# A scan feeding a routed expert layer on one core: weights loaded in smaller transfers, and four pieces of work placed later in the program

## The chip, the core and the metric

The kernel runs on one core of a Trainium2 chip. The metric is the device time of one execution in microseconds (us), and the smaller number is better. Three executions of the kernel before took 277.38, 278.45 and 274.22 us, so the median is 277.38 us.

## The reference, cut to what matters

Two layers follow each other. The first is a chunked linear scan over 768 positions for 4 batches and 8 heads, with a state of 16 x 32 per head:

```python
for c in range(nc):
    cum = np.cumsum(la, axis=-1)
    L = np.exp(cum[:, :, :, None] - cum[:, :, None, :]) * causal
    M = np.einsum('bhin,bhjn->bhij', Cc, Bc) * L
    y_intra = np.einsum('bhij,bhjd->bhid', M, xc)
    y_inter = np.einsum('bhin,bhnd->bhid', Cc, state) * np.exp(cum)[:, :, :, None]
    y[:, :, sl] = y_intra + y_inter
    state = decay_full * state + sum_j(Bc * xc * decay_from_j)
```

Its output is laid out as 3072 tokens of 256 numbers. The second layer sends every token to one of 8 experts by a cosine score, and runs that expert's two matrices:

```python
logits = normalized(x) @ normalized(expert_emb).T / tau
expert_idx = np.argmax(logits, axis=1)
gate_w = softmax(logits)[expert_idx]
for e in range(E):
    mask = expert_idx == e
    h = np.maximum(x[mask] @ w1[e], 0.0)        # 256 -> 1024
    out[mask] = gate_w[mask, None] * (h @ w2[e]) # 1024 -> 256
```

All of it is in float32.

## The kernel before, in words

**First layer, function `mamba`.** The positions are cut into 6 chunks of 128; a chunk with 2 of the 4 batches is a pair, so there are 12 pairs, and the loop `for i in range(2, NP)` (line 478) takes one pair an iteration, in an order that is written out by hand and kept as written on every engine. In iteration `i` the matrix engine (PE) spreads the decays of pair `i+2` (L270), multiplies B by C of pair `i` (`inner`, L329), turns the outputs of pair `i-2` into tokens with their scores (`finish`, L404), adds up states (L292), and makes the outputs of pair `i-1` (`outputs_before` L362, `outputs_within` L377). VectorE (DVE) multiplies C by the decays (`scale_c`, L281: it reads the PSUM tile `pz` that `finish` writes next), masks the products (`keep_inner`, L338), and picks the experts (`pick`, L626 to L635; `locate`, L654 to L658, gives each token its row). GpSimd (POOL) writes tokens to their experts' rows in HBM by indirect DMA (`scatter`, L669), up to four a call.

The decays of chunks 4 and 5 are computed by the generator `decays` (L111), whose five portions run on DVE: one before the loop (L476) and one at the end of each of iterations 2 to 5 (L526). The second portion's result is turned at iteration 5 (`turn_decays`, L141), and the last portion's is needed at iteration 6 (`between`, L149).

**Second layer, function `moe`.** Each expert has 416 places for tokens (4 tiles of 104), in rows in HBM. Expert 0 is treated apart: its first 208 places, from chunks 0 to 3, are the early tokens (`load_early`, tile `xe`), multiplied with `up` (L831) while the last tokens are still being scattered, at the end of `mamba` (lines 535 to 549). `moe` (lines 1108 to 1118) then runs `down` (L848) for the early tokens, `out` (L862, then an indirect DMA from POOL, L869), then `part(1)`, the other 208 places of expert 0 (tile `xg`), and then `part(2)` to `part(8)`, one for each of experts 1 to 7. These seven use a scheme with seven products instead of eight (class `Seven`). It needs mixtures of the weights, made on POOL by four additions of 128 x 512 each (L890): `mix_up` for the first matrix and `mix_down` for the second. A copy into the tile `tick` (L1103) makes POOL wait for the gate of the current part before it mixes.

`prepare` (L789 to L800) turns scores into gates: nine small DVE instructions and one exponential on ScalarE (ACT). It is called for the early tokens at the end of `mamba` (L549), ahead of `down`.

`leftover_blocks` (L1121 to L1176) lays out blocks for tokens beyond an expert's 416 places: 23 DVE instructions, all issued between `out` of the early tokens and `part(1)`. `leftover` (L1179) runs such blocks later if there are any.

**PSUM in `up` and `down`.** A tile `sum` has 5 buffers (L823). In `up`, odd `f` are evacuated by DVE (`hT`, L837) and even `f` by ACT (L835). `down` for `j = 0` reads `hT` of `f = 0, 1, ... 7` in turn.

**Weights.** Each expert has `w1` (1 MB) and `w2` (1 MB), in pools of 3 buffers. `load_w1` (L226) issues four transfers from the sync engine (SP), each to 32 partitions with two runs of 4 KB each; `w2` is one transfer to 128 partitions. All loads are issued from SP, whose queue is in program order: the loads of `mamba`, weights of experts 0 and 1 (L488), `xe` (waits for the last scatter of chunk 3), weights of expert 2 (L527), and the two `xg` (wait for the last scatter of all).

Of the kernel before, what the change touches and what calls it, by code (L numbers as in the profile page):

```python
# [24 lines left out]
TR, NT = 104, 4  # L25
# [199 lines left out]

def load_w1(k, t, w1):  # L226

    w = w1.rearrange("(t j o d) f -> o t d j f", t=2, j=2, o=2)
    for o in range(2):
        for i in range(2):  # L230
            p = 32 * (2 * o + i)
            k.nc.sync.dma_start(t[p : p + 32], w[o, i])


def load_weights(k, e):
    k.w1t[e] = k.wp.tile([128, KD, F], F32, name="w1", tag="w1")
    load_w1(k, k.w1t[e], k.w1[e])
    k.w2t[e] = k.wp.tile([128, KF, DM], F32, name="w2", tag="w2")
    k.nc.sync.dma_start(k.w2t[e][:], k.w2[e].rearrange("(f p) m -> p f m", p=128))


def pair(k, p):
# [122 lines left out]
            )  # L365


def outputs_within(k, p):

    c, b, t = pair(k, p)  # L370
    s = k.un[p]
    for i in range(2):
        for q in range(4):
            for v in range(2):
                n = 32 * (4 * v + q)
                o = 64 * (q % 2) + 32 * v
                k.nc.tensor.matmul(  # L377
                    half_of(k, p, q // 2, i)[o : o + 32, :], lhsT=s.x[:, i, n : n + 32], rhs=s.g[i][:, q, v, :],
                    start=(c == 0 and i == 0), stop=True, tile_position=(0, o), skip_group_check=True,
                )  # L380
# [36 lines left out]
def mamba(k):  # L417
    k.f = k.mc.tile([128, 2, Q], F32, name="f")
    k.r = k.mc.tile([128, 2, Q], F32, name="r")
    k.rT = k.mc.tile([128, 2, 128], F32, name="rT")  # L420
    k.parts = k.mc.tile([128, 2, 2, 4], F32, name="parts")
    k.tick = k.const.tile([1, 1], F32, name="tick")
    k.sides = k.mc.tile([128, NB, 2, 8], F32, name="sides")
    k.whole = k.mc.tile([128, 2, NB, NC - 1], F32, name="whole")
    k.old, k.V, k.yT, k.to = {}, {}, {}, {}
    k.dec = [decays(k, kk) for kk in range(2)]
    NP = NU // 2
    load_decays(k)
    load(k, 0)
    load_emb(k)  # L430
    build_consts(k)
    load(k, 1)
    load(k, 2)
    fill_rows(k)
    load(k, 3)
    for _ in range(4):
        next(k.dec[0])
    turn_decays(k, 0, k.py[:, 384:512])

    for p in range(2):  # L440
        spread_f(k, p)
        scale_c(k, p)
        if p:
            next(k.dec[0])
        else:
            measure_emb(k)
        scale_x(k, p)
    scale_x(k, 2)
    sums(k, 0)
    spread_f(k, 2)  # L450
    scale_c(k, 2)
    scale_emb(k)

    inner(k, 0)
    sums(k, 1)
    between(k, 0, k.pf[:, 256:288])
    turn_emb(k)
    spread_f(k, 3)
    for j in range(2):
        keep_inner(k, 0, j)  # L460
    states(k, 0)
    join(k, 0, k.pf[:, 256:288])
    next_states(k, 0)
    scale_x(k, 3)
    scale_c(k, 3)
    route_consts(k)
    inner(k, 1)
    sums(k, 2)
    sums(k, 3)
    outputs_within(k, 0)  # L470
    for j in range(2):
        keep_inner(k, 1, j)
    keep_outputs(k, 0)
    states(k, 1)
    scale_x(k, 4)
    next(k.dec[1])  # L476

    for i in range(2, NP):
        new = i + 2 if i + 2 < NP else None
        out, done = i - 1, i - 2  # L480
        c = (i + 2) // 2

        pick_now = (i - 3) // 2 if i % 2 else None
        place_now = i // 2 - 2 if i % 2 == 0 and 4 <= i else None
        if i % 2 == 0 and i // 2 + 3 < NC:
            load(k, i // 2 + 3)
        if i in (6, 2 * EC + 2):
            load_weights(k, len(k.w1t))  # L488
        if new is not None:
            spread_f(k, new)  # L490
            scale_c(k, new)
        inner(k, i)
        if i == 5:
            turn_decays(k, 1, k.py[:, 384:512])
        if i == 6:
            between(k, 1, k.py[:, 304:336])
            join(k, 1, k.py[:, 304:336])
        if place_now is not None:
            locate(k, place_now)
            if place_now == EC - 1:  # L500
                count_early(k)
        for j in range(2):
            keep_inner(k, i, j)
        if place_now == EC - 1:
            split_early(k)
            scatter(k, place_now, 0, NB, None)
            load_early(k)
        elif 4 <= i < 2 * EC + 2:
            scatter(k, (i - 4) // 2, 2 * (i % 2), 2, done)
        if i % 2 == 0 and i // 2 < NC - 1:  # L510
            next_states(k, i // 2)
        finish(k, done)
        keep_tokens(k, done)
        if new is not None and c < NC - 1:
            sums(k, new)
        outputs_before(k, out)
        outputs_within(k, out)
        keep_outputs(k, out)
        if pick_now is not None:
            pick(k, pick_now)  # L520
        if new is not None and i % 2 and c < NC - 1:
            states(k, c)
        if new is not None and new + 1 < NP:
            scale_x(k, new + 1)
        if i < 6:
            next(k.dec[1])  # L526
    load_weights(k, len(k.w1t))  # L527
    last = NP - 1
    outputs_before(k, last)
    outputs_within(k, last)  # L530
    locate(k, NC - 2)
    finish(k, last - 1)
    keep_outputs(k, last)
    keep_tokens(k, last - 1)
    j = k.early[0]
    j.turn_x(k.pf[:])
    finish(k, last)
    keep_tokens(k, last)
    scatter(k, NC - 2, 0, NB, None)
    pick(k, NC - 1)  # L540
    sums_at = (k.pz[:, 0, :], k.pf[:], k.pg[:, 0, :])
    for f in range(KF):
        j.up(f, sums_at[f % 3])
        if f == 2:
            locate(k, NC - 1)
            scatter(k, NC - 1, 0, NB, None)
            j.measure()
    count(k)
    j.prepare(k.early_has[:TR, 0, :])  # L549


def route_consts(k):
# [486 lines left out]
def moe(k):  # L1039
# [13 lines left out]
    def part(i):  # L1053
# [14 lines left out]
        if isinstance(j, Seven):  # L1068
            portions = j.measures()
            for f in range(KF // 2):  # L1070
                j.up(f)
                out(f)
                if not new:
                    next(portions)
                if not new and f == KF // 2 - 1:

                    k.nc.gpsimd.drain()  # L1077
            j.up(KF // 2, new.turn_x if new else None)
            if not new:
                j.mix_h((1, 0))  # L1080
                j.down_last(lambda: j.prepare(has))
                return
            j.mix_h()
            turn()
            j.down(lambda: j.prepare(has), (lambda: leftover(k)) if i == n - 3 else None)
        else:
            for f in range(KF):
                j.up(f)
                out(f - 1)
                if f == 3:  # L1090
                    j.measure()
                    parts[EE + 1][0].mix_down()
            new.turn_x()
            turn()
            j.prepare(has)
            j.down(0, j.nt)
# [11 lines left out]
    with k.tc.manual_schedule():  # L1108
        begin(EE)
        begin(EE + 1)  # L1110
        parts[EE + 1][0].mix_up()
        parts[0][0].down(0, HT)
        parts[1][0].turn_x()
        parts[1][0].turn_copies()
        parts[0][0].out(0, HT)
        leftover_blocks(k)
        for i in range(1, n):
            part(i)


def leftover_blocks(k):  # L1121
# [15 lines left out]
    n_i = tile_("n_i", [128, E], I32)  # L1137
    nc.vector.tensor_scalar(out=n_i[:], in0=over[:], scalar1=float(Q - 1), scalar2=None, op0=ALU.add)
    nc.vector.tensor_single_scalar(n_i[:], n_i[:], 7, op=ALU.arith_shift_right)
    nb = tile_("nb", [128, E])  # L1140
    nc.vector.tensor_copy(out=nb[:], in_=n_i[:])
    zero = tile_("zero", [128, E])
# [2 lines left out]
    nc.vector.tensor_tensor_scan(out=end[:], data0=nb[:], data1=zero[:], initial=0.0, op0=ALU.add, op1=ALU.add)  # L1145
    begin = tile_("begin", [128, E])
    tt(begin[:], end[:], nb[:], ALU.subtract)


    be = [128, LEFT, E]  # L1150
# [6 lines left out]
    def of(name, v):  # L1157
# [2 lines left out]
        nc.vector.reduce_sum(out=r[:], in_=tmp[:], axis=AX.X)  # L1160
        return r

    ef = of("left_e", k.step[:, 0:E])
    bf = of("left_b", begin[:])
    nf = of("left_n", over[:])
    tt(bf[:], k.step[:], bf[:], ALU.subtract)
    nc.vector.tensor_scalar_mul(bf[:], bf[:], float(Q))
    tt(nf[:], nf[:], bf[:], ALU.subtract)
    rf = tile_("left_r", [128, LEFT])
    nc.vector.tensor_scalar(out=rf[:], in0=ef[:], scalar1=float(T), scalar2=float(CAP), op0=ALU.mult, op1=ALU.add)  # L1170
    tt(rf[:], rf[:], bf[:], ALU.add)
# [2 lines left out]
    nc.vector.tensor_copy(out=table[:, 1, 0:1], in_=end[:, E - 1 : E])  # L1174

    k.left = table, rf, nf  # L1176


def leftover(k):  # L1179
# [4 lines left out]
    with k.tc.If(blocks > 0):  # L1184
        with k.tc.For_i(0, blocks, 1) as i:
            e = nc.values_load(table[0:1, 0, bass.ds(i, 1)], engines=(SP,), min_val=0, max_val=E - 1)
            w1 = k.wp.tile([128, KD, F], F32, name="w1", tag="w1")
            load_w1(k, w1, k.w1[bass.ds(e, 1)].rearrange("o k f -> (o k) f"))
            w2 = k.wp.tile([128, KF, DM], F32, name="w2", tag="w2")
            nc.sync.dma_start(w2[:], k.w2[bass.ds(e, 1)].rearrange("o (f p) m -> p (o f) m", p=128))  # L1190
            j = Job(k, 1, Q, w1, w2)
# [108 lines left out]
```

## Time and profile before

| what | value |
| --- | --- |
| three executions | 277.38, 278.45, 274.22 us |
| the profiled execution | 274.61 us, of which 272.9 us are the span from the first to the last instruction |
| busy, share of the span | PE 91%, DVE 70%, POOL 61%, ACT 37% |
| moved by DMA | 38.88 MB, mean 142 GB/s |
| first layer | 0 to about 78 us; a pair about every 4.4 us from 56 us on |
| early tokens: `up`, `down` | PE 81.7 to 87.5 us, 87.5 to 93.4 us |
| `part(1)`: `up`, `down` | PE 96.6 to 102.2 us, 102.9 to 112.3 us |
| `part(2)` and those after it | from 112.1 us, about 21.6 us each |

Engines are named PE (matrix), PEld (weight load of PE), DVE, ACT, POOL, SP. L848 is line 848 of the kernel; `sum<-hT,w` reads as "writes `sum`, reads `hT` and `w`". A view of waits names who waited for whom and for how long in all. A timeline gives start, duration, engine, line, operation and shapes, and in brackets the idle time before it and what ended it. The page's row of digits cuts the span in 40 slices of 6.8 us; PEclk is the clock granted to PE in tenths of full speed.

### The profile page before, as it was taken

Reading aid. Unit: us, or ns where it says so; the run is one execution under the profiler, and the core shown is the slowest. Engines: PE = TensorE matmul, PEld = TensorE weight load, DVE = VectorE, ACT = ScalarE, POOL = GpSimd, SP = SyncE. Lnnn points to the kernel's source line nnn. Section 1 sums busy time; section 2 is a strip of 40 time slices with the busy share of each in tenths; the row PEclk is TensorE's granted clock in tenths of the full one; section 3 lists DMA queues with packets and bytes.
Section 4 is the critical chain, followed back from the end, with each engine's and each line's share of the span. In section 5 each row is a group of like instructions: output and inputs, shape, how many; then the busy total and the mean of one; then the engine's idle time right before and its main releaser. Section 6 shows DMA issues by size and latency. Waiting matters only on the chain. (4 is left out here: it accounts for less than half of the span.)

```text
span 272.9 us, 5956 instructions
## 1 busy us (share of the span) xinstructions
PE 247.7 (91%) x2133; PEld 226.4 (83%) x2133; DVE 192.4 (70%) x545; ACT 99.6 (37%) x313; POOL 166.1 (61%) x230
## 2 busy tenths in 40 slices
PE   1997997999989795999999999999999999999990
PEld 0786776778779694999999999999999989998880
DVE  6788794689734589468768767867866866965950
ACT  2512452044336031245244354345344325425310
POOL 4354172447537975791598499499589679525224
PEclk9997997599999999999999999999999999999997
DMA  5989999941269427347435544562670120102002
GB/s 182 374 348 346 397 212 284 215 138 64 83 150 302 151 57 154 113 111 184 133 91 141 146 144 101 137 195 64 152 220 14 45 72 0 53 4 61 0 4 60
DMA packets 19364, 38.88 MB, mean 142 GB/s; under 512 B 2509, under 2 KB 10906, under 8 KB 19333
## 3 DMA queue, kind: packets, MB, share of 16 engines
q1 hardware_dynamic: 16469, 31.94, 41.5%
q0 software_dynamic: 2688, 6.50, 7.4%
q8 instruction: 17, 0.28, 0.4%
q14 instruction: 14, 0.11, 0.1%
q10 hardware_dynamic: 176, 0.06, 0.1%
HBM read 28.37 MB, written 10.37 MB: 142 GB/s over the span
## 5 line engine op out<-in xcount | busy, mean ns | idle before, releaser
L869 POOL DMA_INDIRECT out_dram<-yo,to x32 | 39.4, 1231 | 13.7 <-issue 4.2
L921 DVE TENSOR_TENSOR part<-sum,part 128x208 f32<-128x208 f32 x69 | 25.6, 371 | 25.4 <-ACT part L926 21.4
L913 PE MATMUL sum<-dx,m 128*128 128x208 f32 x168 | 40.4, 351 | 0.7 <-DVE part L921 0.7
L669 POOL DMA_INDIRECT rows<-yt,row_of x24 | 24.1, 1002 | 27.2 <-DVE row_of L658 10.5
L890 POOL TENSOR_TENSOR m<-w 128x512 f32<-128x512 f32 x28 | 35.6, 1272 | 0.5 <-PE sum L913 0.3
L921 DVE TENSOR_TENSOR h<-sum,part 128x208 f32<-128x208 f32 x84 | 29.2, 370 | 8.2 <-PE sum L913 5.2
L913 PEld LDWEIGHTS sum<-dx,m 128*128 128x128 f32 x168 | 29.1, 189 | 4.7 <-DVE part L921 4.2
L913 PE MATMUL sum<-dh,m 128*128 128x208 f32 x168 | 30.8, 339 | 0.0
L338 DVE TENSOR_TENSOR g<-pg,mask 128x1024 f32<-128x1024 f32 x24 | 28.2, 1218 | 3.2 <-PE pg L329 3.2
L913 PEld LDWEIGHTS sum<-dh,m 128*128 128x128 f32 x168 | 29.7, 190 | 0.0
L913 PE MATMUL sum<-xT,w 128*128 128x208 f32 x112 | 27.6, 339 | 0.0
L926 ACT COPY part<-sum 128x208 f32<-128x208 f32 x42 | 14.0, 332 | 27.7 <-PE sum L913 27.7
L913 PE MATMUL sum<-h,w 128*128 128x208 f32 x112 | 20.8, 339 | 0.0
L329 PE MATMUL pg<-cm,bt 32*128 32x256 f32 x192 | 20.8, 461 | 0.0
L966 ACT ACTIVATE h<-h 128x208 f32<-128x208 f32 x28 | 10.6, 377 | 26.8 <-DVE h L921 26.8
L781 POOL TENSOR_TENSOR gr<-gr,half 104x4 f32<-104x4 f32 (+1 forms) x9 | 9.6, 1064 | 17.5 <-ACT sq L775 17.5
L913 PEld LDWEIGHTS sum<-h,w 128*128 128x128 f32 x112 | 19.8, 190 | 0.0
L913 PEld LDWEIGHTS sum<-xT,w 128*128 128x128 f32 x112 | 19.5, 190 | 0.0
L890 POOL TENSOR_TENSOR m<-m,w 128x512 f32<-128x512 f32 x14 | 17.9, 1277 | 1.1
L890 POOL TENSOR_TENSOR m<-w,m 128x512 f32<-128x512 f32 x14 | 17.9, 1276 | 0.0
L957 ACT ACTIVATE h<-h 128x208 f32<-128x208 f32 x28 | 10.6, 377 | 18.2 <-DVE h L921 18.2
L404 PE MATMUL pz<-turn,yT 128*128 128x136 f32 x88 | 14.9, 319 | 2.3 <-DVE cp L281 1.8
(235 smaller groups left out, 526.0 us busy)
## 6 DMA issues: line engine op xcount, KB each, us to landing
w<-in_moe_w_dram SPq DMA_DIRECT2D x32, 256.0 KB
w<-in_moe_w_dram SPq DMA_DIRECT2D x8, 1024.0 KB
rows<-none SPq DMA_DIRECT2D x8, 442.0 KB
xg<-rows SPq DMA_DIRECT2D x7, 442.0 KB
x<-in_x_dram SPq DMA_DIRECT2D x6, 512.0 KB
ct<-in_CT_dram SPq DMA_DIRECT2D x6, 256.0 KB
bt<-in_BT_dram SPq DMA_DIRECT2D x6, 256.0 KB
b<-in_B_dram SPq DMA_DIRECT2D x6, 256.0 KB
```

The costliest lines, as they stand in the source:

```text
L329: nc.tensor.matmul(k.pg[:, q, 256 * i : 256 * i + 256], lhsT=t.bt[r, b + i, :], rhs=s.cm[r, i], start=True, stop=True, tile_position=(32 * ...
L338: k.nc.vector.tensor_tensor(out=g[:], in0=k.pg[:, :, 256 * i : 256 * i + 256].rearrange("p q (t i) -> p q t i", t=2), in1=k.mask[:].unsque ...
L404: k.nc.tensor.matmul(token_psum(k, p, i)[:, at : at + Y1], lhsT=yT[:, j, i, :], rhs=k.turn[:, j, :], start=(j == 0), stop=(j == 1), skip_g ...
L669: d = nc.gpsimd.indirect_dma_start(out=k.rows[:, :], out_offset=bass.IndirectOffsetOnAxis(ap=k.to[g][:, u : u + 1], axis=0), in_=k.yt[:, N ...
L781: nc.gpsimd.tensor_tensor(out=s.r[:], in0=s.r[:], in1=k.half[0:tr, 0:nt], op=ALU.pow)
L869: d = nc.gpsimd.indirect_dma_start(out=k.out[:, :], out_offset=bass.IndirectOffsetOnAxis(ap=s.to[:, i : i + 1], axis=0), in_=y[:], in_offs ...
L890: s.k.nc.gpsimd.tensor_tensor(out=out, in0=in0, in1=in1, op=op)
L913: s.k.nc.tensor.matmul(ps, lhsT=lhsT(i, g), rhs=rhs(j, g), start=(first and g == gs[0]), stop=(g == gs[-1]), skip_group_check=True,)
L921: s.k.nc.vector.tensor_tensor(out=out, in0=in0, in1=in1, op=ALU.add)
L926: s.k.nc.scalar.copy(out=out, in_=ps)
L957: nc.scalar.activation(o[:, 3], o[:, 3], ACT.Relu)
L966: nc.scalar.activation(o[:, 2], o[:, 2], ACT.Relu)
```

## The change

Five things move or are cut differently.

1. `load_w1` issues four transfers to 64 partitions with one run of 4 KB each, in place of 32 partitions with two. `w2` goes in four transfers of 256 KB (two of its eight column blocks each) in place of one. The transfers of experts 0 and 1 are issued in portions of two in iterations 5 to 11. SP does nothing but issue, so what counts there is its order: in the new program `xe` stands after `w1` of expert 1 and ahead of `w2` of expert 1; everything else keeps its order.
2. The portions of the later decays run after `keep_inner` of iterations 2, 3, 4 (one each) and 5 (two), where they ran ahead of the loop and at the ends of iterations 2 to 5.
3. At the end of `mamba`, `locate` of chunk 4 stands between the two halves of the last `outputs_within`, and `finish` and `keep_tokens` of the last pair stand ahead of the turning of the early tokens `xe`.
4. `prepare` of the early tokens stands after their `down` and ahead of `out`; `out` stands ahead of the turning of `xg`; `mix_up` of expert 1 stands after `out`, behind a `tick` copy that waits for the gate, where it stood ahead of `down`.
5. `leftover_blocks` is a generator of eight portions, and one portion runs after each `f` of `up` in `part(1)`. On DVE the order becomes: three instructions, `hT` of f=1, seven, `hT` of f=3, the two small ones of `measure`, four, `hT` of f=5, five, `hT` of f=7, four. `mix_down` of expert 1 stays at `f == 3` of the same `up`.

```diff
 def load_w1(k, t, w1):
-    w = w1.rearrange("(t j o d) f -> o t d j f", t=2, j=2, o=2)
+    w = w1.rearrange("(t j o d) f -> o j t d f", t=2, j=2, o=2)
     for o in range(2):
-        for i in range(2):
-            p = 32 * (2 * o + i)
-            k.nc.sync.dma_start(t[p : p + 32], w[o, i])
+        for j in range(2):
+            k.nc.sync.dma_start(t[64 * o : 64 * o + 64, j, :], w[o, j])
+            yield
+
+def weights(k, e):
+    k.w1t[e] = k.wp.tile([128, KD, F], F32, name="w1", tag="w1")
+    yield from load_w1(k, k.w1t[e], k.w1[e])
+    k.w2t[e] = k.wp.tile([128, KF, DM], F32, name="w2", tag="w2")
+    w2 = k.w2[e].rearrange("(f p) m -> p f m", p=128)
+    for f in range(0, KF, 2):
+        k.nc.sync.dma_start(k.w2t[e][:, f : f + 2, :], w2[:, f : f + 2, :])
+        yield
...
-    next(k.dec[1])
+    first = (None for e in range(2) for _ in weights(k, e))
     for i in range(2, NP):
...
-        if i in (6, 2 * EC + 2):
-            load_weights(k, len(k.w1t))
+        if i >= 5:
+            for _ in range(2):
+                next(first)
...
         for j in range(2):
             keep_inner(k, i, j)
+        for _ in range(1 if i < 5 else 2 if i == 5 else 0):
+            next(k.dec[1])
...
-        if i < 6:
-            next(k.dec[1])
-    load_weights(k, len(k.w1t))
+    for _ in first:
+        pass
+    load_weights(k, 2)
     last = NP - 1
     outputs_before(k, last)
-    outputs_within(k, last)
+    outputs_within(k, last, (0,))
     locate(k, NC - 2)
+    outputs_within(k, last, (1,))
     finish(k, last - 1)
     keep_outputs(k, last)
     keep_tokens(k, last - 1)
+    finish(k, last)
+    keep_tokens(k, last)
     j = k.early[0]
     j.turn_x(k.pf[:])
-    finish(k, last)
-    keep_tokens(k, last)
...
     count(k)
-    j.prepare(k.early_has[:TR, 0, :])
...
                 if f == 3:
                     j.measure()
                     parts[EE + 1][0].mix_down()
+                next(blocks)
+            for _ in blocks:
+                pass
...
         begin(EE)
         begin(EE + 1)
-        parts[EE + 1][0].mix_up()
-        parts[0][0].down(0, HT)
+        j, has = parts[0]
+        j.down(0, HT)
+        j.prepare(has)
+        j.out(0, HT)
         parts[1][0].turn_x()
         parts[1][0].turn_copies()
-        parts[0][0].out(0, HT)
-        leftover_blocks(k)
+        k.nc.gpsimd.tensor_copy(out=k.tick[:], in_=j.gate[0:1, 0:1])
+        parts[EE + 1][0].mix_up()
+        blocks = leftover_blocks(k)
```

The rest of the diff puts `yield` into `leftover_blocks` and lets `outputs_within` take its halves.

More of the change, by code (lines that the diff above doesn't have):

```diff
@@ L226, in load_w1 @@
 def load_w1(k, t, w1):
-    w = w1.rearrange("(t j o d) f -> o t d j f", t=2, j=2, o=2)
+    w = w1.rearrange("(t j o d) f -> o j t d f", t=2, j=2, o=2)
     for o in range(2):
-        for i in range(2):
-            p = 32 * (2 * o + i)
-            k.nc.sync.dma_start(t[p : p + 32], w[o, i])
+        for j in range(2):
[9 more added lines that the diff above has]
+        yield
 def load_weights(k, e):
[L236 to L239, printed above, removed]
+    for _ in weights(k, e):
+        pass
 def pair(k, p):
@@ L365, in outputs_before, with outputs_within @@
             )
-def outputs_within(k, p):
+def outputs_within(k, p, units=(0, 1)):
     c, b, t = pair(k, p)
     s = k.un[p]
-    for i in range(2):
+    for i in units:
         for q in range(4):
@@ L1092, in part @@
                     parts[EE + 1][0].mix_down()
+                next(blocks)
+            for _ in blocks:
+                pass
             new.turn_x()
@@ L1139, in leftover_blocks @@
     nc.vector.tensor_single_scalar(n_i[:], n_i[:], 7, op=ALU.arith_shift_right)
+    yield
     nb = tile_("nb", [128, E])
@@ L1147, in leftover_blocks @@
     tt(begin[:], end[:], nb[:], ALU.subtract)
+    yield
     be = [128, LEFT, E]
@@ L1161, in of @@
         return r
+    yield
     ef = of("left_e", k.step[:, 0:E])
+    yield
     bf = of("left_b", begin[:])
+    yield
     nf = of("left_n", over[:])
+    yield
     tt(bf[:], k.step[:], bf[:], ALU.subtract)
@@ L1168, in leftover_blocks @@
     tt(nf[:], nf[:], bf[:], ALU.subtract)
+    yield
     rf = tile_("left_r", [128, LEFT])
@@ L1176, in leftover_blocks @@
     k.left = table, rf, nf
+    yield
 def leftover(k):
@@ L1187, in leftover @@
             w1 = k.wp.tile([128, KD, F], F32, name="w1", tag="w1")
-            load_w1(k, w1, k.w1[bass.ds(e, 1)].rearrange("o k f -> (o k) f"))
+            for _ in load_w1(k, w1, k.w1[bass.ds(e, 1)].rearrange("o k f -> (o k) f")):
+                pass
             w2 = k.wp.tile([128, KF, DM], F32, name="w2", tag="w2")
```

## The prediction

> **What bounds the kernel now.** I read the page first (busy shares, row of digits), then PE's waits, then timelines around each wait, then windows of 2 us for the clock.
>
> From the page:
>
> ```profile
> PE   1997997999989795999999999999999999999990
> ...
> PEclk9997997599999999999999999999999999999997
> ```
>
> PE is nearly full from the 17th slice on (about 115 us), where the seven experts run at 21.6 us each. Nothing that the change touches lies on their path. What can be won or lost lies before 115 us: PE's gaps, and the two dips of the clock. The gaps, from PE's view of waits:
>
> ```profile
> PE sum L848 <- DVE hT L837: 3.3, 1, 3.3
> ...
> PE py L362 <- issue: 2.0, 1, 2.0
> PE turned L809 <- DMA xg<-rows: 2.0, 1, 2.0
> PE pz L404 <- DVE cp L281: 1.8, 1, 1.8
> PE pf L809 <- DMA xe<-rows: 1.1, 1, 1.1
> ```
>
> The change aims at four of the five (all but "issue"). The largest, at 103.4 to 106.7 us, has this on DVE:
>
> ```profile
> 102.34 0.39 DVE L1160 TENSOR_REDUCE left_n<-mine_not 128x28 f32<-128x224 f32 x1
> 102.64 0.84 DVE L1130 TENSOR_TENSOR left_b<-step,left_b 128x28 f32<-128x28 f32 x1
> 103.51 1.18 DVE L1167 TENSOR_SCALAR left_b<-left_b 128x28 f32<-128x28 f32 x1
> 104.72 1.19 DVE L1130 TENSOR_TENSOR left_n<-left_n,left_b 128x28 f32<-128x28 f32 x1
> 105.84 0.17 DVE L1170 TENSOR_SCALAR left_r<-left_e 128x28 f32<-128x28 f32 x1
> ```
>
> and this on POOL:
>
> ```profile
> 100.79 1.26 POOL L890 TENSOR_TENSOR m<-w 128x512 f32<-128x512 f32 x1
> 102.13 1.30 POOL L890 TENSOR_TENSOR m<-m,w 128x512 f32<-128x512 f32 x1
> 103.40 1.25 POOL L890 TENSOR_TENSOR m<-w 128x512 f32<-128x512 f32 x1
> 104.62 1.25 POOL L890 TENSOR_TENSOR m<-w,m 128x512 f32<-128x512 f32 x1
> ```
>
> The reader is to see that DVE instructions of 28 elements, 0.2 us by themselves, last about 1.2 us and end just as a POOL addition ends; the reduction does not. Beside four POOL additions DVE gets one such instruction through per addition. The clock, by windows:
>
> ```profile
> 38.00:40.00 2.00, 2.00 (x35) 1.44 (x32) 1.62 (x3) 1.38 (x4) 1.81 (x5) 1.00 1.03 219
> 40.00:42.00 2.00, 0.38 (x8) 0.14 (x8) 1.97 (x3) 0.28 (x1) 1.76 (x3) 1.00 1.04 192
> 44.00:46.00 2.00, 2.00 (x19) 2.00 (x20) 1.09 (x5) 0.69 (x3) 0.00 (x0) 0.50 1.07 388
> 52.00:54.00 2.00, 2.00 (x40) 1.59 (x36) 1.07 (x2) 0.00 (x0) 1.52 (x2) 0.50 1.11 202
> ```
>
> After the "issue" gap at 40.4 us the clock is 0.50 until 54 us (last three columns: clock, DMA share, GB/s).
>
> **What the Trainium skill says.** "SBUF — State Buffer", section "Who interferes with whom": a DVE instruction with two SBUF inputs, or in a two-port mode, is blocked for the whole of a GpSimd instruction that reads SBUF, while reductions never are. The trace agrees (1.18 us against 0.39 us above). The same page, "Door 1: The DMA port swizzle": 1 MiB to partitions 0..31 went at 189 GB/s and to 0..63 at 196, since both reach the same 8 ports. The trace shows `w1` at 196 to 219 GB/s, other loads at 391 (30 to 34.5 us). "Runtime: NRT & Kernel Launch", "Instruction fetch mechanics": instructions come by DMA in blocks of 16 KiB, 256 of them. The trace agrees: its instruction queue has 17 packets with 0.28 MB, and PE has 4266 instructions, 16.7 blocks. One packet began at 39.57 us amid `w1`, and PE ran dry at 40.38 us in the midst of a batch. "TensorE: Matmul & The Clock Gate", "What's actually happening": PE's clock halves or returns by its activity in windows of 3.4 us. The trace's half-clock stretches are 3.4 and 10.2 us long.
>
> **The change part by part.**
>
> *Later decays.* The first portion lies on DVE at 21.33 to 22.99 us, ahead of the `cp` that PE waits for (23.45 us). Behind the masks it frees `cp` by about 1.6 us. DVE's work stays, so PE gains only what DVE had idle soon after: 1.01 and 0.39 us ahead of L281 and L338 at 28.1 and 28.9 us. I take -1.5; ends 0 and -1.8. The deadlines hold: the second portion's result is turned two iterations later.
>
> *Weights.* By the 196 against 189 GB/s of the skill, `w1` (5.2 us at 200 GB/s) shrinks by 0.2 us, off PE's path: 0. If it went at 391 GB/s, two loads would be 2.6 us shorter each, also off the path except through instruction fetches (rival 1). SP issues three more transfers an expert, some 1.3 us by 0.4 us each, ahead of the next `xg`. That one is issued at 112.86 us for a turn at 122.08 us, so several us cover it: 0. `w2` of expert 1 now follows `xe`, 1 MB or 2.8 us more of DMA at 77 to 92 us, amid the scatters whose end releases `xg`. `xg` may land up to 1 us later: 0 to +1, mostly absorbed, since POOL sets the end below.
>
> *Last outputs.* PE's 1.09 us wait for `xe` is filled by `finish` (1.11 us), but `up` doesn't start sooner. `xe` lands at 80.29 us as before (its scatters and SP's order ahead of it are unchanged), then turn 0.57, the rest of the `yt` copy (0.6) ahead of it on ACT, and the `xT` copy 0.51 give 81.7 us; before 81.65: 0. `locate` is 0.5 us earlier, and four scatters with it, but the last four wait for chunk 5's `row_of`, behind `f == 2` of `up`: 0.
>
> *The early part's end and the blocks.* PE ends `down` at 93.39 us.
> 1. DVE: `yoT` to 93.8; `prepare` 1.80 (the late tokens' at 109.00 to 110.80, no POOL beside it) to 95.6; `yo` 0.47 to 96.1. `xg` lands at 95.4, turn 0.57; its two copies, now behind `yo`, 0.66 to 96.7. `up` starts at 96.75; before 96.55. Before, most of `prepare` ran under `down`; that cover is gone.
> 2. PE: `up` 5.8 to 102.5, turn to 103.3.
> 3. POOL: the two output DMAs begin 0.33 after `yo` and need 1.07 and 0.31 between: 96.45 to 98.9. `tick` 0.2, `mix_up` 4 x 1.29 from 99.15 to 104.3, pow 0.75, `mix_down` to 110.3. Before, `mix_up` ran at 91 to 96 us, where PE did not need DVE.
> 4. DVE: `hT`(1) at 98.7. From 99.15 us ten instructions with two SBUF inputs or in a two-port mode come ahead of `hT`(7): three `mine`, `gl`, three `mine_not`, three on `left_b` and `left_n`. Nine POOL instructions stand beside them. One each: `hT`(3) at 103.45, `hT`(5) at 107.35, and `hT`(7) after POOL's last, 110.3 + 0.2 + 0.37 = 111.0 us (rounded up for starts).
> 5. PE: `down` runs to f=4 (105.2), waits 2.1, runs f=5 and 6 (108.1), waits 2.9. After `hT`(7) nine pairs of 0.35 remain: 114.2 us; before 112.25: +1.95.
> 6. The next part's `dx` and gates are then 4 us later on DVE (about 113.1 and 114.9 us), and its first addition waits some 0.3 us: +0.3.
>
> Ends: if POOL never held DVE, `hT`(7) would come by 105.1 us and `down` end at 103.3 + 5.6 = 108.9: -3.35. The other end is +3, with `xg` late.
>
> *Sum.* -1.5 + 1.95 + 0.3 = +0.75. Against the profiled execution: 274.61 + 0.75 = 275.4 (span 273.65, 1.7 around it). The median shown is 2.77 above the profiled one, so by the median it is 278.1. I take the middle, 276.8 us.
>
> **The rivals.**
>
> *Rival 1: the stalled instruction fetch is missed.* With PE 1.5 us ahead, the block that came late (39.57 us) may be asked for before `w1` fills the queues at 34.8 us; the block at 29.99 us, amid 391 GB/s, stalled nobody. It saves 2.04 us and the half clock: PE's pair at 43.87 to 54.34 takes 10.5 us, where a bound by DVE (6.0 us busy) would be about 5.8, so 4.7. Together -6.7: 270.1 us. Against: the two `w1` loads still fill about 10 of the 20 us, and PE at full clock needs a block every 4.5 us, so another block can be late.
>
> *Rival 2: POOL does not hold DVE*, and the interleaving gives what it seems to promise: 276.8 - 2.25 - 3.35 = 271.2 us. Against: four of four instructions above were held.
>
> *Rival 3, slower: the clock drops in the early part.* PE would be idle for 5 of 5.8 us at 105.2 to 111.0. At 40.4 us a gap of 2.04 us was followed by three half-clock windows. Three windows from 111 us (10.2 us) cost 5.1: 281.9; four cost 6.8: 283.6 us. It decides once a window has clearly less PE work than at 102 to 105 us in the profile shown (about 1.7 of 3.4 us, all 128 rows), which did not lower the clock.
>
> That the change doesn't do what it says is no rival for the orders, but is for `w1`: "more partitions" brings no more ports.
>
> **How the numbers follow.** The forecast 0.47 (own range 273 to 281), rival 1 0.25, rival 2 0.10, rival 3 0.18. Over 2% is under 271.8 or over 282.9 us, about what a measurement of this kernel can tell from no change. Faster: four fifths of rival 1 and six tenths of rival 2, 0.26. Slower: six tenths of rival 3 and 0.04 of the forecast's tail, 0.15. Same: 0.59. The range 268.5 to 283 takes in all four cases.
>
> **What would show it.** Right: no wait of L404 for `cp` near 22 us; DVE's block instructions at about 1.2 us beside POOL between 99 and 110 us; PE waiting for `hT` twice, near 105 and 108; the experts from about 114 minus 1.5 us. Wrong: short block instructions, `down` of `part(1)` ending before 109 us, or clock 1.00 throughout 35 to 56 us (rival 1).

## The result and the profile after

The changed kernel takes 370.31 us (median of 4 executions, 368.85 to 371.49), the kernel before in the same comparison 277.91 us. The ratio is 1.342, with a 95% interval of 1.326 to 1.359. All ratios here leave out executions more than 1.5% above the fastest of their kernel, and the medians keep them, so a ratio can differ a little from that of two medians. The forecast of 276.8 us and its whole range were missed by far. The profiled execution took 371.03 us, with a span of 369.3 us.

The page of the changed kernel, its slices of 9.2 us for PE, the granted clock and the DMA engines:

```profile
PE   3998899900970789149924990699099619999992
...
PEclk9999999955696699859985997599769968999998
DMA  6999262262154003501350145023302510200101
```

Before, PE was full from 115 us on, where seven experts ran one behind the other. Now PE has a hole between two experts, but for the last of them, and the clock falls behind each hole. From the fifth slice on the DMA engines are seldom more than half busy, although 38.88 MB have to be moved as before. PE's view of waits says what it waits for in the holes (microseconds in total, times, longest):

```profile
PE turned L821 <- DMA xg<-rows: 70.2, 6, 13.2
PE pf L821 <- DMA xe<-rows: 18.4, 1, 18.4
...
PE sum L860 <- DVE hT L849: 1.5, 1, 1.5
...
PE pz L413 <- DVE cp L290: 0.5, 1, 0.5
```

The two token loads cost 88.6 us, 85.5 more than before, and PE's own busy time rose from 247.7 to 261.1 us, together with a lower clock (mean 0.866, before 0.968). 85.5 and 13.4 are 98.9 us; the span grew by 96.4. Two of the small waits at which the other edits aimed, for `hT` (3.3 us before) and for `cp` (1.8), are smaller than before, as the last two lines show. So the loss is late tokens, and the clock that falls while PE waits for them.

Why are they late? The timeline of the sync engine's queue gives start, duration and the number of issues in the row. Before, four issues of a `w1` took 1.7 us:

```profile
123.79 1.72 SPq L232 DMA_DIRECT2D w<-in_moe_w_dram  x4
```

Now the issues are stuck:

```profile
73.82 12.76 SPq L242 DMA_DIRECT2D w<-in_moe_w_dram  x4
86.62 9.76 SPq L231 DMA_DIRECT2D w<-in_moe_w_dram  x4
96.43 15.27 SPq L242 DMA_DIRECT2D w<-in_moe_w_dram  x4
111.94 3.36 SPq L759 DMA_DIRECT2D xg<-rows  x2
131.03 3.90 SPq L231 DMA_DIRECT2D w<-in_moe_w_dram  x4
```

The first two `xg` loads stand behind 38 us of weight issues. (`xe` does not: it was issued at 72.6 us, before 77.2, and still landed late, as is shown below.) What blocks the issues is seen in windows of 1 us. Behind the length of the window stand busy time and count of PE, PEld, DVE, ACT and POOL; the last three columns are the clock, the DMA share and GB/s. First the changed kernel, at a time when the four transfers of a `w1` have all been issued (by 134.93 us) and nothing else moves:

```profile
136.00:137.00 1.00, 1.00 (x7) 1.00 (x7) 0.99 (x5) 0.00 (x0) 0.00 (x0) 1.00 0.13 37
137.00:138.00 1.00, 1.00 (x8) 1.00 (x7) 0.87 (x6) 0.00 (x0) 0.00 (x0) 1.00 0.13 41
```

Then the kernel before, as it loads a `w1`:

```profile
126.00:127.00 1.00, 1.00 (x7) 1.00 (x6) 1.00 (x2) 0.00 (x0) 0.00 (x0) 1.00 0.99 221
127.00:128.00 1.00, 1.00 (x8) 1.00 (x7) 0.90 (x2) 0.00 (x1) 0.00 (x0) 1.00 1.11 242
```

The share is the mean over 16 DMA engines. 0.13 of 16 is 2: the same `w1` that kept all engines busy is now moved by two of them, at 37 to 41 GB/s. At that pace its 1.05 MB take 26 to 28 us, and an expert's work on PE takes 21.6.

### The profile page after: what moved, and what is told of

Same layout as the page of the kernel before. It is cut to its first block, busy times and chain, and to the rows that moved or that the text cites. A ratio compares the mean times of both kernels' runs of the same rounds, so it can differ in the third digit from the quotient of the medians.

```text
span 369.3 us, 5995 instructions
## 1 busy us (share of the span) xinstructions
PE 261.1 (71%) x2133; PEld 237.7 (64%) x2133; DVE 189.4 (51%) x545; ACT 100.4 (27%) x313; POOL 160.5 (43%) x231
## 2 busy tenths in 40 slices
DMA packets 19300, 38.88 MB, mean 105 GB/s; under 512 B 2445, under 2 KB 10842, under 8 KB 19269
## 5 line engine op out<-in xcount | busy, mean ns | idle before, releaser
L821 PE MATMUL turned<-ident,xg 104*128 104x104 f32 x60 | 10.8, 349 | 70.2 <-DMA xg<-rows 70.2
L821 PEld LDWEIGHTS turned<-ident,xg 104*128 104x128 f32 x60 | 8.9, 201 | 72.0 <-issue 58.5
L881 POOL DMA_INDIRECT out_dram<-yo,to x32 | 33.4, 1044 | 18.8 <-DVE yo L877 10.3
L978 ACT ACTIVATE h<-h 128x208 f32<-128x208 f32 x28 | 10.6, 377 | 91.9 <-DVE h L933 91.8
L925 PE MATMUL sum<-h,w 128*128 128x208 f32 x112 | 25.9, 395 | 0.0
L925 PEld LDWEIGHTS sum<-h,w 128*128 128x128 f32 x112 | 25.4, 236 | 0.4
L338 PE MATMUL pg<-cm,bt 32*128 32x256 f32 x192 | 19.9, 443 | 0.0
```

The costliest lines, as they stand in the source:

```text
L338: nc.tensor.matmul(k.pg[:, q, 256 * i : 256 * i + 256], lhsT=t.bt[r, b + i, :], rhs=s.cm[r, i], start=True, stop=True, tile_position=(32 * ...
L821: nc.tensor.transpose(s.xp[j][:, tr * i : tr * i + tr], s.x[:, i, Y1 * j : Y1 * j + 128], k.ident[:tr, :tr])
L881: d = nc.gpsimd.indirect_dma_start(out=k.out[:, :], out_offset=bass.IndirectOffsetOnAxis(ap=s.to[:, i : i + 1], axis=0), in_=y[:], in_offs ...
L925: s.k.nc.tensor.matmul(ps, lhsT=lhsT(i, g), rhs=rhs(j, g), start=(first and g == gs[0]), stop=(g == gs[-1]), skip_group_check=True,)
L978: nc.scalar.activation(o[:, 2], o[:, 2], ACT.Relu)
```

## Theory and rivals

The Trainium skill, page "DMA: Bandwidth & Descriptors", section "Why a DMA increments its semaphore by 16 and not by 1", has a rule for it: a transfer is spread over k engines, where k is the largest number up to 16 that divides the size of the slowest dimension (sizes of 1 apart) of both access patterns. The new pattern of `w1` is `t d f`, and its slowest dimension is `t`, of size 2. The old one was `d j f`, with 32. The section "Rules for kernel authors" on that page says the same as a warning, about an outermost dimension under 16.

**Theory.** The source pattern confines `w1` to 2 of 16 engines. Everything else that is spread over all 16 waits for its parts on these two.

**Rivals.** (1) Transfers to 64 partitions with one run of 4 KB each are slow in themselves. (2) The portions and their order are: more issues, `xe` ahead of a `w2`, `xg` behind more weights. (3) One of the other edits is.

## Experiments

**The old source in the changed kernel, and the new source in the kernel before.** The first run undoes nothing but the source of `w1`:

```diff
 def load_w1(k, t, w1):
-    w = w1.rearrange("(t j o d) f -> o j t d f", t=2, j=2, o=2)
+    w = w1.rearrange("(t j o d) f -> o t d j f", t=2, j=2, o=2)
     for o in range(2):
-        for j in range(2):
-            k.nc.sync.dma_start(t[64 * o : 64 * o + 64, j, :], w[o, j])
+        for i in range(2):
+            p = 32 * (2 * o + i)
+            k.nc.sync.dma_start(t[p : p + 32], w[o, i])
             yield
```

> The changed kernel with one thing undone: w1 is fetched as before (four transfers of 32 partitions with two runs of 4 KB each, whose source has a slowest dimension of 32). Portions, order, decays, outputs and blocks stay as changed. Theory (the source pattern of w1, with a slowest dimension of 2, confines each transfer to 2 of the 16 DMA engines): all of the loss goes, 270 to 280 us; packets of 4096 B have 13 to 16 in flight; PE's waits for xg and xe fall from 88.6 us to under 6. Rival portions or order (16 more issues, xe ahead of the second w2, xg behind more weight issues): stays above 310 us with xg waits of 40 us or more. Rival other edits (decays, outputs, blocks): stays above 340 us.

Measured: 278.85 us, ratio to the kernel before 0.990 (0.986 to 0.994). PE's waits for `xg` fall, and `xe` is not waited for:

```profile
PE turned L822 <- DMA xg<-rows: 1.5, 2, 1.3
```

(The expected 13 to 16 packets in flight did not come: the mean is 11.0, and 11.3 in the kernel before, so that count stays below 16 even where all engines work.) The second run makes only this edit, the other way round, in the kernel before:

> The kernel before with one thing changed: w1 is fetched by the new four transfers (64 partitions each, source slowest dimension 2). w2 goes as one transfer, nothing else moves. Theory (two engines): 340 to 375 us, packets of 4096 B 1 to 3 in flight, PE waits mostly for xg and w1. Rival portions or order: at most 285 us. Rival other edits: at most 280 us.

Measured: 372.66 us, ratio 1.327 (1.318 to 1.337). Its waits are those of the changed kernel:

```profile
PE turned L808 <- DMA xg<-rows: 72.4, 6, 13.1
PE pf L808 <- DMA xe<-rows: 13.0, 1, 13.0
```

So the edit of `load_w1` is the whole of the loss, and rivals 2 and 3 fall: it costs some 92 us alone, and without it all other edits together cost nothing.

**How many engines.** Three runs keep the changed kernel, its 64 partitions and its single runs of 4 KB, and change only how many pieces the source has: 4, 8, or one piece of 64 rows.

```diff
-    w = w1.rearrange("(t j o d) f -> o j t d f", t=2, j=2, o=2)
+    w = w1.rearrange("(t j o d) f -> o j t d f", t=4, j=2, o=2)
```

> The changed kernel, with w1 in four transfers of 64 partitions, each from four groups of 16 rows of w1 (slowest dimension of the source 4, not 2). It computes with the rows of w1 in another order than the reference; the work is the same. Theory (as many engines as the slowest dimension): packets of 4096 B twice as many in flight as with 2, some 3 (2.6 to 3.4), w1's MB in about 13 us in place of 26, so that the weights of an expert fit into its 21.6 us of PE: 275 to 300 us. If only a source of 64 rows in one piece is fast (the number of groups does not matter): 340 us or more. If any source of more than two groups is fast: 270 to 278 us with 13 or more packets in flight.

> The changed kernel with w1 from eight groups of 8 rows of w1 each (slowest dimension of the source 8). It computes with the rows of w1 in another order than the reference; the work is the same. Theory (as many engines as the slowest dimension): after 120 us about 6 to 8 packets of 4096 B in flight, between the 4.7 of four groups and the 11.4 of 64 rows; w1 in 6 to 8 us, hidden behind 21.6 us of PE: 276 to 282 us, with no wait for xg over 2 us. If four groups' 293.6 us came from something that does not scale with the groups: 290 us or more.

> The changed kernel, with w1 still in four transfers of 64 partitions with one run of 4 KB per partition, but each from 64 rows of w1 that lie one behind the other, so that the source's slowest dimension is 64 and not 2. It computes with the rows of w1 in another order than the reference; the work is the same. Theory (two engines, because of the source's slowest dimension): 270 to 280 us, 13 to 16 packets of 4096 B in flight. Rival 64 partitions or single runs of 4 KB are slow in themselves: 340 us or more, as changed. Rival portions: above 310 us.

Windows of 1 us in which `w1` alone moves, with four groups and then with eight:

```profile
134.00:135.00 1.00, 1.00 (x7) 1.00 (x7) 0.90 (x2) 0.00 (x0) 0.00 (x0) 1.00 0.25 74
```

```profile
122.00:123.00 1.00, 1.00 (x8) 1.00 (x7) 1.00 (x2) 0.13 (x1) 0.00 (x0) 1.00 0.50 148
125.00:126.00 1.00, 1.00 (x8) 1.00 (x7) 0.97 (x4) 1.00 (x6) 0.00 (x0) 1.00 0.50 176
```

| slowest dimension | DMA share while `w1` moves | in sixteenths | packets of 4 KB in flight after 120 us | time, us | ratio to before |
| --- | --- | --- | --- | --- | --- |
| 2 (changed kernel) | 0.13 | 2 | 2.8 | 370.31 | 1.342 (1.326 to 1.359) |
| 4 | 0.25 | 4 | 4.7 | 293.62 | 1.048 (1.039 to 1.058) |
| 8 | 0.50 | 8 | 7.7 | 271.16 | 0.990 (0.984 to 0.995) |
| 64 | 1.03 to 1.11 | 16 | 11.4 | 278.72 | 0.997 (0.993 to 1.000) |

(The times come from different chips; the ratios are to be compared. The packets are counted from the trace, as a mean over the time in which there are any.) Rival 1 falls: 64 partitions with single runs are as quick as 32 with two, to within 1%. The share is the number of pieces over 16 for 2, 4 and 8, and with 64 it is full. It is the number of engines that falls, not their pace: after 120 us a packet of 4 KB took 197 ns on average in the changed kernel and 259 ns in the kernel before.

The updates of each load's semaphore, which the trace keeps, show the same transfer by transfer. Leaving out one update at the end of an issue, which loads on fewer than 16 engines have, a transfer of `w1` from 2, 4, 8 and 64 pieces has 2, 4, 8 and 16 of them, as data lands. One of `w2` has 16, and a token load of 104 rows has 13. These are the rule's numbers. In the changed kernel 11 of the 13 for `xe` came by 76.6 us and the last two at 90.2 and 91.8 us, just behind the last two of the `w1` issued ahead of it (89.6 and 90.9). A transfer of `w2` issued at 139.2 us has 14 by 142.6 us and two at 157.5 and 158.7. With four pieces it is four that come late. So the transfers of `w1` all use the same engines, and what is spread over more is complete only when its part there is done.

Eight pieces are enough here: 148 to 197 GB/s bring a `w1` in an estimated 5 to 7 us, hidden behind 21.6. PE still waited once, 3.7 us, for the first `xg`, where at most 2 were expected. Four, at 74 to 98 GB/s and an estimated 11 to 14 us, would by themselves be hidden too; still `xg` was waited for 16.8 us in six waits, since its last parts come behind `w1`.

**By which way it reaches PE.** Here the source stays at 2, and only the token loads go to another queue:

```diff
-        return s.k.nc.sync.dma_start(x[:].rearrange("p t w -> p (t w)"), rows)
+        return s.k.nc.scalar.dma_start(x[:].rearrange("p t w -> p (t w)"), rows)
```

> The changed kernel with its new source of w1, and the loads of xe and xg issued from ACT's queue and not behind the weights in SP's. If the wait is one of SP's queue (the loads are issued late): the 88.6 us of waits for xg and xe fall by half or more, 290 to 330 us. If the two engines are the bound (w1's MB takes 26 us on them, with their share of everything else 30 to 35 us per expert, against 21.6 us of PE): 360 to 375 us, the waits for xg only renamed (to w1, or xg landing as late as before).

Measured: 328.09 us, ratio 1.196 (1.188 to 1.204): inside the range recorded for the queue, at its upper end, and far from all of the loss. The wait for `xg` is gone, and waits for ACT have come:

```profile
PE pz L413 <- ACT yT L399: 33.5, 1, 33.5
PE sum L925 <- ACT part L938: 12.7, 3, 4.9
...
PE turned L821 <- DMA xg<-rows: 0.8, 1, 0.8
```

The first is this run's own loss. ACT stood still before it could issue `xe`:

```profile
ACT yt L421 <- issue: 37.0, 1, 37.0
```

The scatters that `xe` needs had landed by 72.6 us, but the wait ended at 98.6 us, when a transfer of expert 2's `w1` landed that is counted on the same semaphore as `xe`. So the gain of the other queue is understated by the total, and is better read from the experts.

By the start of each expert's `dh` on DVE, experts with weights still to load follow each other in 34 to 36 us in the changed kernel and in 27 to 28 us here (the first step, 21.5 us, has its weights from before). So of some 14 us lost per expert, about 7 belong to SP's queue, where `xg` stands behind stuck weight issues. The 6 or 7 that remain are the weights themselves: POOL waits 3.0 to 4.1 us for `w1` and starts to mix at 191.4, 219.7 and 248.0 us, within 0.3 us of the landing of its last transfer, ACT waits 5.6 to 6.7 us for weights beside it, and 27 to 28 us are about what two engines need for a `w1`. The token loads themselves hardly suffer from ACT's queue: their last two updates come some 3 to 4 us behind the others.

**The other edits, each alone in the kernel before.** They test the recorded steps one by one.

> The kernel before with the portions alone: w2 in four transfers, the weights of the first two experts issued two transfers per iteration from the sixth on (the second expert's w2 so behind xe); w1 keeps its old source. Recorded prediction: 0 to +1 us beside before (277 to 279 us). If portions or order cost what the changed kernel lost: over 300 us. If issuing from the sixth iteration on, in pieces, spares PE the stall at 40 us: 270 to 275 us, clock 1.00 through 35 to 56 us.

Measured: 281.69 against 281.81 us, ratio 0.999 (0.994 to 1.004): nothing, as recorded.

> The kernel before with the decays of the second chunk group behind the masks alone. Recorded prediction: -1.5 us (ends 0 and -1.8), the wait for cp near 22 us gone, so 275.5 to 277.5 us. Rival instruction fetch (PE's stall at 40 us with the half clock behind it is missed): 270 to 272 us and clock 1.00 through 35 to 56 us. Rival too late: the decays' turn waits for DVE, 278 us or more.

Measured: 280.54 against 281.81 us by the medians, ratio 0.983 (0.978 to 0.989).

> The kernel before with the last outputs ahead of the early tokens alone. Recorded prediction: 0 us; PE's wait for xe (1.1 us) is filled, but the first up-projection starts at 81.7 us as before. If xe's wait sets the end: -1 us.

Measured: 279.87 against 281.81 us by the medians, ratio 0.988 (0.985 to 0.992).

> The kernel before with the end of the early part alone: prepare and out behind down, the mix of the late part behind them, the further tokens' blocks in portions between the hT steps. Recorded prediction: +2.25 us (POOL's additions hold DVE's small instructions at 1.2 us each, hT waits at 105 and 108 us, the down-projection of the first full part ends near 114.2 us, before 112.25). Rival POOL does not hold DVE: -3.35 us, block instructions at 0.2 to 0.4 us. Rival clock: +5 us or more with half clock after 111 us.

Measured: 284.55 against 281.81 us, ratio 1.011 (1.005 to 1.017): about +3 us, near the recorded +2.25.

> The kernel before with the later decays and the last outputs alone (w1's old source, old order of weights, old end of the early part). If the two gains measured alone (ratios 0.983 and 0.988) add up: a ratio near 0.972. If both are one and the same gain (less half clock and fewer stalls ahead of 60 us, given back at the same later wait): near 0.985.

Measured: 273.71 against 274.56 us by the medians, ratio 0.995 (0.992 to 0.999). Both edits together gain less than each seemed to alone. Executions of one kernel spread by 3% and more (the kernel before took 271.21 to 281.18 us beside this run). I take no more than 1% as shown for either, and their sum as 0.5%.

**A better version.** In the kernel before, 9.5 us of block instructions lie ahead of `hT`. This run takes decays and outputs, and moves the blocks behind `part(1)`, one DVE instruction after each `up` step of the next four parts:

```diff
                 j.up(f)
                 out(f)
+                if i < 6:
+                    next(blocks, None)
...
-        leftover_blocks(k)
+        blocks = leftover_blocks(k)
```

> As the kernel with decays and outputs alone, and the further tokens' blocks not ahead of hT but one DVE instruction after each step of the up-projection of the next four parts, where DVE waits 0.8 us per step for PE. Theory (the 9.5 us of block instructions, held by POOL, are what hT waits for, 3.3 us in the kernel before): the hT wait goes and the time falls by 2 to 3.5 us beside it. Rival (hT comes as late for another reason, xg or its copies): no difference. Other side: an instruction held by POOL for 1.3 us delays the sums and PE waits in each of 16 steps, up to 8 us more.

Measured: 270.82 us beside 273.71, ratio to before 0.988 (0.984 to 0.992). The wait for `hT` is gone. DVE's rows show `hT` as soon as PE has its sum, 1.4 us apart (the first two of four):

```profile
94.68 0.38 DVE L837 TENSOR_SCALAR hT<-sum 128x208 f32<-128x208 f32 x1 [1.26 <-PE sum L831]
96.09 0.38 DVE L837 TENSOR_SCALAR hT<-sum 128x208 f32<-128x208 f32 x1 [1.03 <-PE sum L831]
```

From the early tokens' `yoT` to that of `part(1)` it takes 13.4 us (91.8 to 105.3), in the run with decays and outputs alone 19.7 (92.3 to 112.0). Two more runs add the portions:

> The changed kernel without the new source of w1 and without the new end of the early part: decays, outputs and portions. Portions measured alone made no difference (0.999), so as the run beside it; if portions spare PE the stall at 40 us, 1 per cent less; if xe's neighbour transfers delay xg, up to 1 us more.

> Decays, outputs and portions of the changed kernel, w1's old source, the old end of the early part, and the further tokens' blocks one DVE instruction at a time in the next four parts. If the portions' gain beside decays and outputs (0.9867 against 0.9952) and the later blocks' (0.9879) add up: a ratio near 0.980. If both fill the same wait (PE waited 4.2 us for xg with portions): as the better of the two, 0.986 to 0.989.

Measured: 270.60 us, ratio 0.987 (0.982 to 0.992), without the later blocks, and 271.32 us, 0.988 (0.983 to 0.993), with them. The gains do not add, and the traces have a reason. With decays and outputs alone PE waits 1.6 us for the first `xg` and 3.3 us for `hT`; with the later blocks 1.7 us for `xg` and not for `hT`; with the portions 4.2 us for `xg` and not for `hT`; with both 4.3 us for `xg`. With the portions the second expert's `w2` follows `xe`, the last scatter takes 5.5 us to land in place of 2.8, and `xg`, which waits for it, is issued at 92.1 and 93.2 us in place of 89.1. Behind that later `xg` the blocks no longer make `hT` late, so moving them has nothing left to remove. Why the portions help beside decays and outputs (0.987 against 0.995) was not settled. Three versions are so about 1.2% faster than the kernel before, and none is told from the others.

## Why the prediction was wrong

**What bounds the kernel.** Right for the kernel before. But "Nothing that the change touches lies on their path", said of the seven experts, was wrong: `w1` of every expert passes through `load_w1`, and 21.6 us per expert is a cover only for a load that is shorter. A load of 26 to 28 us is not.

**The step that failed is "Weights".** It put `w1` at 0.2 us less, "off PE's path: 0"; the runs show two of 16 engines and 26 to 28 us for each `w1`, where 5.2 were taken (at 200 GB/s; the prediction's own rows have 192 to 219). I priced the new shape by the partitions at its destination (196 against 189 GB/s) and never by the pattern at its source, for which the skill has the rule quoted above. The term measures about +92 us, by the run with the new source alone (372.66 us at a ratio of 1.327). The bound from both sides, 391 GB/s at one end, had no slow end at all: no profile row showed a transfer whose source is in two pieces, and there I should have left room for a loss. The same step took SP's issues at 0.4 us each. In the changed kernel four took up to 15.3 us; with it falls the sentence ahead of the prediction that only SP's order counts. For the second `w2` behind `xe` it had `xg` up to 1 us late; with the old source it is issued about 3 us later (92.1 against 89.4 us with and without the portions), and the portions alone cost nothing (0.999), as recorded. The remark that the change may not do what it says "for `w1`" looked at the right line for the wrong reason.

**Decays (recorded -1.5 us).** The wait for `cp` went from 1.8 to 0.5 us in the changed kernel, and the fifth `cp` starts at 21.5 us, before at 22.9, so the place is right: 1.4 us, where 1.6 were recorded. "The deadlines hold" was not quite right: spreading the decays reads `f`, which a later portion writes, and PE now waits for that portion, where it did not before:

```profile
PE pz L279 <- DVE w L132: 1.0, 1, 1.0
```

That takes most of what the wait for `cp` gave. The size of the whole is not settled: a ratio of 0.983 alone, 0.995 together with the outputs.

**Last outputs (0).** PE does not wait for `xe` in the run with this edit alone, as recorded. The ratio, 0.988, would be 3 us of gain, the medians 1.9, both edits together 0.5%: not told from the recorded values with certainty.

**Early part's end and the blocks (+2.25).** Mechanism right, sizes off. In the changed kernel itself late tokens hide it. The run with the old source shows it on DVE:

```profile
101.59 1.12 DVE L1149 TENSOR_TENSOR begin<-end,nb 128x8 f32<-128x8 f32 x1
102.75 1.42 DVE L1149 TENSOR_TENSOR mine<-begin,step 128x224 f32<-128x224 f32 x1
104.08 1.46 DVE L1149 TENSOR_TENSOR mine_not<-end,step 128x224 f32<-128x224 f32 x1
105.58 2.04 DVE L1149 TENSOR_TENSOR mine<-mine,mine_not 128x224 f32<-128x224 f32 x1
107.54 0.36 DVE L850 TENSOR_SCALAR hT<-sum 128x208 f32<-128x208 f32 x1
```

Beside them POOL's instructions follow each other, additions of 1.25 to 1.43 us and one of 0.87:

```profile
101.38 1.31 POOL L903 TENSOR_TENSOR m<-m,w 128x512 f32<-128x512 f32 x1
102.64 1.27 POOL L903 TENSOR_TENSOR m<-w 128x512 f32<-128x512 f32 x1
103.87 1.43 POOL L903 TENSOR_TENSOR m<-w,m 128x512 f32<-128x512 f32 x1
105.25 0.87 POOL L794 TENSOR_TENSOR gr<-gr,half 104x2 f32<-104x2 f32 x1
106.12 1.25 POOL L903 TENSOR_TENSOR m<-w 128x512 f32<-128x512 f32 x1
```

The four DVE instructions took 6.0 us, one per addition or worse: the last lies beside two POOL instructions, where the skill's sentence in the prediction speaks of one. In the kernel before, with no POOL addition beside them, the four take 0.17 to 0.39 us each. The place where the estimate fell short is `hT`(3): recorded 103.45, measured 107.54 us, since four instructions and not three were held, and `hT`(1) came 2.1 us later (1.0 of them because `down` of the early tokens ended at 94.4 us and not at 93.4). `hT`(5) and `hT`(7) came at 110.8 and 112.7 (107.35 and 111.0). In the run with this edit alone the four last as long to 0.01 us. With the old source PE waits 4.4 us for `hT` in three waits, where 5.0 in two were recorded, and `yoT` of `part(1)` starts at 116.6 us; its `down` was recorded to end at 114.2.

**The rivals.** Rival 1 (the missed fetch stall): in the profile of the run with the decays alone the clock is full through 35 to 56 us and the last `cp` comes at 60.7 us and not at 64.6, so the stall can move. But of these 4 us only 1.3 are left when `up` of the early tokens starts (80.4 us against 81.7). The two profiles come from different chips, where the kernel before took 281.81 and 277.91 us, so where the rest went cannot be told from them. A block of instructions "every 4.5 us" was the shortest spacing: after 55 us they came 4.4, 8.0 and 6.8 us apart. That the stall is a late fetch remains the prediction's reading, and no run tests it. Rival 2 (POOL does not hold DVE) falls by the rows above. Rival 3 named the clock as the cost of the early part's end; the clock fell, to 0.866, but behind the waits for tokens. No rival named the source pattern: the 0.15 for a slower kernel lay on the clock and on the tail of the forecast, and none of it on what happened.

## What to carry to other kernels

When the access pattern of a transfer changes, look at the slowest dimension of both its sides, the source too: 2 pieces there meant 2 of 16 DMA engines, 37 to 41 GB/s for a load that had 221 to 242. A load "off the path" needs a bound from the slow side against its cover, here 21.6 us per expert. The mark of it in a profile is a DMA share that stands at a sixteenth's multiple (0.13, 0.25, 0.50) while loads are waited for, and issues on the sync engine that last for microseconds.

## What the runs showed of the hardware that was not expected

- A transfer of 256 KB on two engines does not only come late itself. Issues behind it on the same queue took up to 6.7 us each (at most 0.5 before). Transfers on that queue that are spread over more engines had their last two updates up to 16 us behind the others. On other queues the delay was smaller: some 3 to 4 us for token loads from ACT's queue and for POOL's scatters, which landed after a median of 5.9 us (3.9 before).
- Moving a wait between queues moved who stands still: ACT waited 37.0 us before it could issue one load, for the landing of a weight transfer counted on the same semaphore, and the ratio to the kernel before still fell from 1.342 to 1.196.
- Holding of DVE by POOL reaches further than one addition: an instruction of 0.39 us by itself took 2.04 us, beside POOL instructions of 0.87 and 1.25 us.
